# Two broadcast matmuls on 128 rows of the array, later zeroing of the state copies, and an earlier weight load, in a fused linear-attention and SiLU-MLP kernel

## The chip, the cores and the metric

The kernel runs on one core of a Trainium2 chip. The metric is device time in microseconds (us) for one execution of the whole kernel. Times inside an execution come from its hardware profile and count from the start of its span. TensorE is PE in the profile (PEld is its weight load), VectorE is DVE, ScalarE is ACT, GpSimd is POOL, and SyncE, which issues most transfers, is SP. A trailing q (ACTq, POOLq) marks the queue of an engine that issues a DMA.

## The reference, cut to what matters

```
B, H, S, D = 4, 8, 768, 48            # r, k, v: (B, H, S, D); w, u: (H, D)
for t in range(S):
    cur   = outer(u * k[t], v[t])                 # the bonus of the present step
    y[t]  = r[t] @ (state + cur)
    state = w * state + outer(k[t], v[t])         # per head, 48 x 48
x = y with its heads side by side                 # (3072, 384)
h = x @ w_in                                      # w_in  (384, 2048)
out = silu(h) @ w_out                             # w_out (2048, 384)
```

## The kernel before

The sequence of each batch is cut into six chunks of 128 steps. A unit is one chunk of one batch, so there are 24 units; unit i is chunk i // 4 of batch i % 4, and units go in pairs. In a chunk the recurrence becomes matrix products: with powers of w multiplied into r and k, `product_pair` forms the 128 x 128 products of r and k for two units (A01, A23, A45 ...), `masked` cuts them to the past, `outputs_y` multiplies with v and adds the carried state, `outputs_s` forms the chunk's contribution to the state, and `state` adds it.

The powers are made once, at the start. `powers_r` and `powers_k` make lamR and lamK (powers of w along time, with head dimensions as partitions). Two row vectors must be copied to all 128 partitions: the bonus factor u, and w. `spread_u` (L193) and `spread_w` (L189) do it as a matmul of a stationary tile of ones with one row: `ones` is 1 x 128 and the moving operand is the one row `u_row` or `w_row`, so that one row of the PE array takes part. `copy_u` brings the result for u to SBUF as u_bc (L196); `ln_w` and `powers_c` make from that for w the factor lamC, with which `decayed_k` scales k (kc).

The bonus term of unit i is made by a chain over POOL and DVE: `bonus_rk` (rk = k*r, POOL, L222), `bonus_rku` (ru = rk*u_bc, POOL, L227), `bonus_sum` (rd, DVE, L235), `bonus_v` (vu, POOL, L240). `evict_y` (DVE, L345) adds vu to the unit's output.

For the first eight units the order of the work on every engine is written out by hand, in the string `order`: each word is one step of one unit, and each engine takes the words that belong to it in this order. `T` turns r and k of a unit (PE, L262), `kT` and `rT` multiply with the powers (DVE, L268), `A` is the product pair (PE, L295), `am` the masking (DVE, L302), `Y` and `S` the outputs (PE, L312, L317, L329), `yT` and `xT` turn the unit's y, `st` puts the state away (DVE). `La.b` and `Ga.b` are pieces of the first MLP matmul and its SiLU (PE L398, ACT L406) with b the first of the 128-wide column blocks of w_in. A word with `n*` ahead of it puts n matmuls on an idle all-zero tile in front (`spin`, L165), whose results nobody reads.

The MLP weights are loaded by POOL-issued transfers that also convert to f16: `ld_win(g)` (L84, words i_q0 to i_q3) brings the g-th quarter of w_in, which holds column blocks 4g to 4g+3; `ld_wout(g)` (L89, i_o0 to i_o3) a quarter of w_out. POOL takes an issue like any other step, in its place in the order. Quarter 3 is needed first by L4.12. In the order before, this stands around the fourth quarter:

```
rk4 v164 L2.4 G2.4 S2 L2.6 G2.6 st2 ru4 i_q3 r164 L4.8 G4.8 S3 T5 ...
```

DVE clears what needs clearing at the start (L102 to L125): wpT, the idle tile, ones, the pads of the first four rin and kin tiles, and the four f16 copies of the state, st16 (`stb` in the profile). st16 is first written by `state` of unit 0.

All PSUM tiles but the two large `att` ones come from one rotation of four buffers (tag `moe`): each new tile waits until the one four places before it has been read.

## Time and profile before

| | |
|---|---|
| time, median of 3 | 190.74 us (190.19 to 191.87) |
| profiled execution | 193.76 us, span 192.0 us, mean granted TensorE clock 0.973 |
| PE busy | 185.3 us (96%) |
| POOL / ACT / DVE busy | 120.2 / 108.5 / 102.8 us |
| bytes moved | 24.16 MB, mean 126 GB/s |

Engine busy times overlap, so they don't add to the span. A busy PE is one with an instruction in flight; how fast this runs depends on the granted clock, which the profile gives as a share of full speed for any stretch. The page cuts the span into 40 slices of 4.8 us; a window view gives the same numbers for stretches that one chooses.

### The profile page before, as it was taken

Reading aid. Unit: us, or ns where it says so; the run is one execution under the profiler, and the core shown is the slowest. Engines: PE = TensorE matmul, PEld = TensorE weight load, DVE = VectorE, ACT = ScalarE, POOL = GpSimd, SP = SyncE. Lnnn points to the kernel's source line nnn. Section 1 sums busy time; section 2 is a strip of 40 time slices with the busy share of each in tenths; the row PEclk is TensorE's granted clock in tenths of the full one; section 3 lists DMA queues with packets and bytes.
Section 4 is the critical chain, followed back from the end, with each engine's and each line's share of the span. In section 5 each row is a group of like instructions: output and inputs, shape, how many; then the busy total and the mean of one; then the engine's idle time right before and its main releaser. Section 6 shows DMA issues by size and latency. Waiting matters only on the chain.

```text
span 192.0 us, 5629 instructions
## 1 busy us (share of the span) xinstructions
PE 185.3 (96%) x2304; PEld 119.5 (62%) x2304; DVE 102.8 (54%) x188; ACT 108.5 (56%) x213; POOL 120.2 (63%) x159
## 2 busy tenths in 40 slices
PE   7899999799999999999999999999999999999993
PEld 2466676578766876665566655656755657644563
DVE  6556888866772673673673574574574364200120
ACT  5747368769370592276791276791376781089300
POOL 8589699999999939839839839839738430000000
PEclk9856999999999999999999999999999999999999
DMA  5999999999569258278168287177287201320022
GB/s 97 200 196 182 213 144 195 219 180 187 115 144 228 85 112 196 66 162 169 44 121 189 64 178 174 28 144 165 71 177 167 44 0 44 82 82 0 3 82 82
DMA packets 90125, 24.16 MB, mean 126 GB/s; under 512 B 83314, under 2 KB 90100, under 8 KB 90100
## 3 DMA queue, kind: packets, MB, share of 16 engines
q1 hardware_dynamic: 84992, 20.39, 49.2%
q0 software_dynamic: 3712, 3.15, 11.2%
q10 hardware_dynamic: 1396, 0.27, 0.7%
q8 instruction: 18, 0.29, 0.6%
q14 instruction: 7, 0.06, 0.1%
HBM read 20.45 MB, written 4.72 MB: 131 GB/s over the span
## 4 chain that ended last, share of the span: by engine, by line
PE 80%; POOL 8%; DMA 6%; issue 3%; ACT 1%; SPq 1%; DVE 0%; POOLq 0%
PE ops L419 32%; PE hps L398 29%; PE att L295 7%; PE att L262 5%; DMA win<-in_moe_w_in_dram 3%; DMA kin<-in_k_dram 2%; POOL kc L230 2%; PE yp L317 2%; POOL rku_f L227 2%; PE yp L312 2%; POOL vu L240 2%; POOL rk L222 1%; PE ops L444 1%; PE sp L329 1%; POOL win L84 1%
## 5 line engine op out<-in xcount | busy, mean ns | idle before, releaser
L398 PE MATMUL hps<-xT,win 128*128 128x512 f16 (+1 forms) x360 | 67.7, 337 | 1.1 <-DMA win<-in_moe_w_in_dram 1.0
L406 ACT ACTIVATE gT<-hps 128x512 f16<-128x512 f32 x96 | 56.1, 598 | 19.5 <-PE hps L398 17.2
L419 PE MATMUL ops<-wout,gT 128*128 128x384 f16 x368 | 64.0, 326 | 0.0
L398 PEld LDWEIGHTS <-win 128*128 128x128 f16 x360 | 33.3, 98 | 24.8 <-DMA win<-in_moe_w_in_dram 1.2
L419 PEld LDWEIGHTS <-gT 128*128 128x128 f16 x368 | 34.7, 98 | 22.2
L240 POOL TENSOR_TENSOR vu<-vin,rku 128x384 f32<-128x384 f32 x24 | 19.7, 828 | 27.7 <-DVE rku L235 27.7
L425 ACT COPY osb<-ops 128x384 f32<-128x384 f32 x20 | 9.6, 478 | 43.4 <-PE ops L419 39.7
L302 DVE TENSOR_TENSOR am<-att,maskM 128x1024 f16<-128x1024 f32 x12 | 14.7, 1225 | 33.3 <-PE att L295 33.3
L227 POOL TENSOR_TENSOR rku_f<-rk,u_bc 128x384 f32<-128x384 f32 x24 | 23.9, 998 | 3.0 <-ACT u_bc L196 1.3
L222 POOL TENSOR_TENSOR rk<-kin,rin 128x384 f32<-128x384 f32 x24 | 24.1, 1003 | 2.0 <-DMA kin<-in_k_dram 1.9
L230 POOL TENSOR_TENSOR kc<-kin,lamC 128x384 f16<-128x384 f32 x24 | 23.9, 1002 | 0.0
L295 PEld LDWEIGHTS att<-rT,kT 48*64 48x64 f32 x768 | 18.6, 141 | 5.1 <-issue 3.7
L268 DVE TENSOR_TENSOR rT<-att,lamR 112x512 f32<-112x512 f32 x24 | 16.5, 686 | 9.7 <-ACT gT L406 4.0
L345 DVE TENSOR_TENSOR y<-yp,vu 128x384 f16<-128x384 f32 x24 | 13.4, 557 | 14.5 <-issue 4.8
L295 PE MATMUL att<-rT,kT 48*64 48x128 f32 (+1 forms) x768 | 20.5, 257 | 0.5 <-DVE rT L268 0.5
L268 DVE TENSOR_TENSOR kT<-att,lamK 112x512 f32<-112x512 f32 x24 | 16.4, 684 | 4.1 <-PE att L262 4.1
L302 DVE TENSOR_TENSOR am<-att,maskX 128x1024 f16<-128x1024 f32 x12 | 14.6, 1215 | 0.0
L340 POOL TENSOR_TENSOR sdec<-st,wCT 112x384 f32<-112x384 f32 x16 | 13.2, 826 | 0.0
L235 DVE TENSOR_REDUCE rku<-rku_f 128x8 f32<-128x384 f32 x24 | 12.2, 545 | 1.6 <-POOL rku_f L227 1.5
L283 ACT CAST rT<-rT 112x512 f16<-112x512 f32 x20 | 12.4, 619 | 0.1
L427 DVE COPY osb<-ops 128x384 f32<-128x384 f32 x3 | 1.7, 557 | 19.7 <-PE ops L419 19.7
L317 PEld LDWEIGHTS <-am 128*128 128x128 f16 x192 | 10.2, 99 | 3.1 <-DVE am L302 1.1
(67 smaller groups left out, 173.7 us busy)
## 6 DMA issues: line engine op xcount, KB each, us to landing
rin<-in_r_dram SPq DMA_DIRECT2D x24, 192.0 KB, 4.1
vin<-in_v_dram SPq DMA_DIRECT2D x24, 192.0 KB, 4.2
kin<-in_k_dram SPq DMA_DIRECT2D x23, 192.0 KB, 4.0
out_dram<-osb SPq DMA_DIRECT2D x23, 192.0 KB, 2.2
win<-in_moe_w_in_dram POOLq DMA_DIRECT2D x4, 384.0 KB, 6.1
wout<-in_moe_w_out_dram POOLq DMA_DIRECT2D x4, 384.0 KB, 7.5
xT<-y SPq DMA_TRANSPOSE x18, 2.3
kin<-in_k_dram ACTq DMA_DIRECT2D x1, 192.0 KB, 4.1
```

What stands on the lines that cost most here:

```text
L222: nc.gpsimd.tensor_tensor(out=L(i)["rk"], in0=kin[i % NIN][:, :, 0:D], in1=rin[i % NIN][:, :, 0:D], op=ALU.mult)
L227: nc.gpsimd.tensor_tensor(out=L(i)["rku_f"], in0=L(i)["rk"], in1=u_bc, op=ALU.mult)
L230: nc.gpsimd.tensor_tensor(out=kc[i % NIN][:, :, 0:D], in0=kin[i % NIN][:, :, 0:D], in1=lamC, op=ALU.mult)
L240: nc.gpsimd.tensor_tensor(out=L(i)["vu"], in0=vin[i % NIN], in1=L(i)["rku"].unsqueeze(2).broadcast_to([128, H, D]), op=ALU.mult)
L268: nc.vector.tensor_tensor(out=L(i)[key].rearrange("p g (y t) -> p y g t", y=2), in0=L(i)["t"][0:PR, :, x], in1=lam.rearrange("p g (y t) -> ...
L295: nc.tensor.matmul(a[e][o0:o0 + HC, j, p, c0:C], kT[r0:r0 + D, p, s0:s0 + HC], rT[r0:r0 + D, p, c0:C], start=True, stop=True)
L302: nc.vector.tensor_tensor(out=am.rearrange("p h g c -> p (h g) c"), in0=L(i)["a"].rearrange("p h g c -> p (h g) c"), in1=(maskX if crossed ...
L317: nc.tensor.matmul(L(i)["y"][:, h, :], L(i)["am"][:, j, p, :], L(i)["vy"][:, h, :], start=not sc, stop=(not sc or j == 1))
L345: nc.vector.tensor_tensor(out=L(i)["y16"], in0=L(i)["y"], in1=L(i)["vu"], op=ALU.add)
L398: nc.tensor.matmul(hps[:, f, :], win[:, q, (ft + f) * 128:(ft + f + 1) * 128], xts[sc][:, q, b0:b0 + nb, :].rearrange("p b t -> p (b t)"), ...
L406: nc.scalar.activation(out=gts[sc][:, ft:ft + m, b0 * C:(b0 + nb) * C], in_=hpss[b0, ft], func=AF.Silu)
L419: nc.tensor.matmul(opss[b], gts[sc][:, ft, b * C:(b + 1) * C], wout[:, ft, :], start=(ft == 0), stop=(ft == NFT - 1))
```

## The change

There are three parts. The broadcast matmuls use all 128 rows of the array: a tile `rows` of 128 partitions is cleared, the two row vectors are loaded into its partition 0, and `ones` becomes 128 x 128, so that 127 rows add zeros. The clearing of the four st16 tiles moves on DVE from before the exponents (eK) to after them. And the issue of the fourth quarter of w_in (i_q3) moves on POOL ahead of rk4 and ru4, the bonus products of unit 4. The first part is meant to make the broadcasts count as full work of the array, the second to make room on DVE for the larger clear, the third to have the weights there earlier.

```diff
-    w_row = cst.tile([1, HD], FP)
-    u_row = cst.tile([1, HD], FP)
-    ones = cst.tile([1, 128], FP)
+    rows = cst.tile([128, 2, HD], FP)
+    ones = cst.tile([128, 128], FP)
...
     nc.vector.memset(idle, 0.0)
+    nc.vector.memset(rows, 0.0)
...
-    nc.scalar.dma_start(out=u_row, in_=bass.AP(tensor=u.tensor, offset=0, ap=[[0, 1], [1, HD]]))
-    nc.scalar.dma_start(out=w_row, in_=bass.AP(tensor=w.tensor, offset=0, ap=[[0, 1], [1, HD]]))
+    nc.scalar.dma_start(out=rows[0:1, 0, :], in_=bass.AP(tensor=u.tensor, offset=0, ap=[[0, 1], [1, HD]]))
+    nc.scalar.dma_start(out=rows[0:1, 1, :], in_=bass.AP(tensor=w.tensor, offset=0, ap=[[0, 1], [1, HD]]))
...
-    for b in range(B):
-        nc.vector.memset(st16[b], 0.0)
...
     def exponents_k():
         nc.vector.tensor_tensor(out=eK, in0=it_row[:, 1:2, :].broadcast_to([PR, NP, C]),
                                 in1=lnwT.unsqueeze(2).broadcast_to([PR, NP, C]), op=ALU.mult)
+        for b in range(B):
+            nc.vector.memset(st16[b], 0.0)
...
-        nc.tensor.matmul(spread["w"], ones, w_row, start=True, stop=True)
+        nc.tensor.matmul(spread["w"], ones, rows[:, 1, :], start=True, stop=True)
...
-        nc.tensor.matmul(spread["u"], ones, u_row, start=True, stop=True)
+        nc.tensor.matmul(spread["u"], ones, rows[:, 0, :], start=True, stop=True)
...
-        rk4 v164 L2.4 G2.4 S2 L2.6 G2.6 st2 ru4 i_q3 r164 L4.8 G4.8 S3 T5 kT5 rT5 L4.9 G4.9 st3
+        i_q3 rk4 v164 L2.4 G2.4 S2 L2.6 G2.6 st2 ru4 r164 L4.8 G4.8 S3 T5 kT5 rT5 L4.9 G4.9 st3
```

## The prediction
> **What bounds the kernel now.** I read the page's slices first, then the granted clock in chosen windows, then the waits of PE, then the timeline around the one long wait. In the slices PE is at 9 nearly everywhere, but the clock row is not:

> ```profile
> PE   7899999799999999999999999999999999999993
> ...
> PEclk9856999999999999999999999999999999999999
> ```

> So PE bounds the kernel from about 21 us to the end: windows from 45 to 160 us show PE busy in every microsecond, at clock 1.00. Ahead of that lie some 10 us at half clock. Cut at the edges of that stretch, the window view (busy time of PE, PEld, DVE, ACT, POOL, then the clock) says:

> ```profile
> 4.50:7.91 3.41, 2.63 (x35) 1.70 (x35) 1.57 (x3) 3.13 (x13) 2.39 (x7) 1.00 1.06 209
> 7.91:11.32 3.41, 3.41 (x47) 2.18 (x49) 1.56 (x3) 2.32 (x5) 2.13 (x3) 0.51 1.04 204
> 11.32:14.74 3.42, 3.42 (x44) 1.67 (x37) 2.61 (x3) 1.01 (x3) 2.56 (x5) 0.50 1.01 174
> 14.74:18.15 3.41, 3.41 (x35) 2.32 (x33) 2.52 (x5) 2.43 (x6) 3.39 (x4) 0.50 1.07 173
> 18.15:21.56 3.41, 2.93 (x64) 1.88 (x65) 2.21 (x4) 1.74 (x4) 1.84 (x3) 0.99 1.26 229
> ```

> The reader is to see that PE was busy for all of 7.9 to 14.7 us by its records and still did not get its clock back. What it ran then is in the timeline, the one-row broadcasts among it:

> ```profile
> 7.52 1.25 PE L193 MATMUL bc<-u_row,ones 1*128 1x384 f32 x2
> ...
> 12.01 1.64 PE L189 MATMUL bc<-w_row,ones 1*128 1x384 f32 x2
> ```

> PE's own waits are short, and the longest after the opening is for w_in. The clock is full there:

> ```profile
> PE hps L398 <- DMA win<-in_moe_w_in_dram: 1.0, 1, 1.0
> ...
> 29.23 0.80 POOL L84 DMA_DIRECT2D win<-in_moe_w_in_dram  x1
> ...
> 35.95 1.47 PE L398 MATMUL hps<-xT,win 128*128 128x512 f16 x6 [1.03 <-DMA win<-in_moe_w_in_dram]
> ```

> That is L4.12 waiting for quarter 3, issued at 29.23 us and, in the chain of waits, under way for 6.68 us. After it PE waits no more. Hence two places where time can come from: the half-clock stretch, and this one wait. The profiled execution took 193.76 us, the timed median is 190.74; I take differences from the trace and put them on the median.

> [...] half clock from 7.95 to about 18.17 us is 10.2 us, three windows of 3.41, at 0.50. [...]

> **The change part by part.**

> *The larger clear.* From 128 elements at 0.165 and 256 at 0.272 an element costs 0.84 ns; 768 elements of rows are 0.165 + 640 x 0.84 ns = 0.70 us, 0.80 if the 256-element row is tripled. I take 0.75. It sits after idle (ends 1.23), so the pad clears that end near 2.47 end near 3.2. The st16 clears (0.84 us, 2.47 to 3.31) leave this place, so DVE is free at 3.2, as before, and eK, which waits for lnwT and starts at 3.56, does not move. ones grows in rows only: 0.165 as before. The four st16 clears now run after eK, 4.25 to 5.1, where DVE is idle until rT0 at 6.21 (1.95 us idle before it). Cost: nothing, hidden by that idle time. First use of st16 is at 25.93.

> *The new wait.* The two row transfers are issued by ACT and must wait for the clear of rows, to about 2.0 us; they were issued at 1.92. Queued behind them on ACT is lnwT at 3.25, which waits for wpT and had ACT idle 1.16 us. A delay of 0.1 to 0.2 passes at most partly into lnwT, lamR and lamK; lamK ends at 5.34, and rT0 needs it at 6.21. Cost nothing. The rows themselves are needed at 7.52.

> *The matmuls.* Same columns, same two passes each. At equal clock I take the same time, ends 0 and, should rows matter, not above the 1.25 us of the u broadcast.

> *What they do to the clock.* Count, per window, the matmuls that cover the array (spins L165, yp L317, yT L383). The window view by line gives: 11.32 to 14.74, spins 1.01 and yp 0.53, so 1.54 us, clock not restored at its end. 14.74 to 18.15: 1.51 + 0.53 + 0.82 = 2.86, clock restored at its end. With the w broadcast counted in full, the first of these has 1.54 + 1.64 = 3.18, more than what sufficed. So the clock comes back one window earlier, at 14.75. For 7.91 to 11.32, 0.61 of spin plus 0.82 of the u broadcast is 1.43, below the 1.54 that did not suffice; and 4.50 to 7.91 gains only 0.4. Those I leave as they are.

> *What one window is worth.* From 14.75 at full clock: am1 ends at 14.95 in any case, Y1 takes 0.37 in place of 0.53 (the eight at 23.40 show it) and ends near 15.4; T2 takes about 0.8 (its like at 18.47 and 18.74), to 16.2; yT0 and yT1 0.33 each, to 16.75; three spins 0.21 each at full clock, T3 from 17.4. It ran from 18.47 before, so kT3 goes from 19.17 to 18.1. The sum of u products rd2 follows at 19.3 in place of 20.38, POOL is free for vu2 from 19.51, and both PE (A23) and POOL (vu2) move ahead by **1.07 us**. Behind this point both engines run without gaps (PE to 34.92, POOL to 29.23), so it carries on.

> *The fourth quarter.* It moves ahead of two POOL products, 27.22 to 29.23: issue 2.03 us earlier. With the same 6.68 us it lands at 33.9, with the slowest POOL-issued median (7.5 us, w_out) at 34.7; PE comes free at 34.92. The 1.03 us wait is gone. But not all of it is gained. am4 can't begin before A45 ends at 34.92; am4 and am5 hold DVE to 37.33, y4 (0.56) and st4 (0.72) to 38.6. yT4 takes the PSUM buffer that st4 reads, so it can't start before about 38.65; it ran at 39.31. **0.66 us** stay; the bounds are 0.6 and 1.03. rk4 and ru4 end 0.8 us later; rd4, behind them, is held by DVE until 33.91 anyway, and i_o0 is not moved. The other transfers of that time are not needed for several us (r and k of unit 6 issued at 22.43 to 29.26, used at 40.4).

> Sum: 1.07 + 0.66 = 1.73, 190.74 - 1.73 = **189.0 us**.

> **Rivals.**
> - *The broadcasts don't count*[...]. Then only the quarter pays: 190.74 - 0.66 = 190.1. For it: A01, f32 too, filled 2.08 us of an unrestored window. Against: its tiles are 48 x 64, so they are also small.
> - *The clock is never lost.* [...] Then u_bc comes 0.6 us earlier, A01 takes about 1.55 in place of 2.84, am0 and rd1 come about 1.3 earlier, and by the same chain kT3 about 2.9 us earlier than now: 190.74 - 2.9 - 0.66 = 187.2. For it: 18.15 to 21.56 kept its clock with 1.00 us of spins and the A23 tiles. Against: transfers run at about 200 GB/s until 36 us and may hold so early a start.
> - *The half clock lands on dense work.* Faster PE work leaves gaps, [...] the next one, 21.6 to 25, runs the MLP at half clock: 3.41 / 2 = 1.7 lost. PE then reaches L4.12 at 36.6 in place of 35.95, the old wait being swallowed: 190.74 + 0.67 = 191.4, slower than before. Against: the 18.15 window held before with less work.

> **How the numbers follow.** The forecast 0.50, broadcasts don't count 0.25, clock never lost 0.15, half clock on dense work 0.10. The range, 187.2 to 190.8, takes the first three with the 0.6 us of run scatter above the second, and leaves the last out. Faster by over 1% means below 188.83: the clock-never-lost case, and not quite half of the forecast[...], together 0.42. Slower by over 1% is above 192.65, which needs the last case and another lost window: 0.06. Within 1%: 0.52.

> **What would show it.** Right: half clock for two windows (about 6.8 us) or fewer; matmul rows for the broadcasts as long as now at the same clock; no wait of L4.12 for win, and a new short PE wait before yT4 behind st4; kT3 about 1 us earlier. Wrong: three half-clock windows at the same places (the rows don't count), a half-clock slice after 21 us, PE still waiting for win (the transfer is bound by bandwidth, not by its issue), or rT0 later than 6.2 us (the opening pays for the clear).

## The result and the profile after

The changed kernel takes 190.05 us (median of 17 runs, 189.33 to 190.67) against 191.48 us for the kernel before (17 runs, 190.18 to 193.72). The ratio is 0.993, with a 95% interval of 0.9907 to 0.9953. So it is faster by 0.7%, clear of noise and below 1%. The forecast of 189.0 us stood on the first median of 190.74 from three runs; over 17 runs the kernel before is 0.74 us longer than that. Comparisons leave the most disturbed runs out, and here the disturbance is the half clock itself, so over all runs the gain is somewhat larger (below).

The page of the changed kernel, its PE and clock rows over the 40 slices:

```profile
PE   7978899999999999999999999999999999999993
...
PEclk9999999999999999999999999999999999999999
```

The same five windows as before the change, columns as there (length, then busy time of PE, PEld, DVE, ACT and POOL, granted clock, DMA share, GB/s):

```profile
4.50:7.91 3.41, 3.27 (x36) 2.06 (x36) 2.35 (x6) 3.13 (x13) 2.63 (x7) 1.00 1.13 226
7.91:11.32 3.41, 3.38 (x69) 2.01 (x67) 2.22 (x4) 2.53 (x6) 2.54 (x3) 1.00 1.12 221
11.32:14.74 3.42, 2.39 (x42) 1.65 (x43) 3.35 (x6) 2.59 (x5) 3.40 (x5) 1.00 1.00 172
14.74:18.15 3.41, 2.93 (x59) 1.77 (x59) 2.54 (x6) 2.39 (x6) 3.31 (x5) 1.00 1.22 211
18.15:21.56 3.41, 2.63 (x59) 2.13 (x52) 3.21 (x4) 1.19 (x2) 3.39 (x5) 1.00 1.10 198
```

Once full, the clock is not lost again; all 17 runs have a mean clock of 0.998 or 1.0. PE is now idle for 1.0 us in the third window where it had been "busy" throughout: at full clock it runs ahead of DVE there, and the longest wait for am is 0.8 us (below). The views read 1.00 from the start, but for the first microseconds this can hardly be so, by the length of two like groups of matmuls in this trace:

```profile
4.93 0.68 PE L262 MATMUL att<-ident,rin 64*112 64x64 f32 x8
...
6.32 0.43 PE L262 MATMUL att<-ident,rin 64*112 64x64 f32 x8
```

The first took what such a group takes at half clock (0.68 us at 15.62 in the trace before, clock 0.50), the second what it takes at full clock. So the full clock begins near 6 us here, and the mean clock of this run, 1.0, doesn't count the opening ahead of that. The timeline, the same rows as before the change, and two that are new:

```profile
1.34 0.70 DVE L103 MEMSET rows<- 128x768 f32 x1
...
6.14 0.69 DVE L268 TENSOR_TENSOR rT<-att,lamR 112x512 f32<-112x512 f32 x1 [1.06 <-PE att L262]
...
7.21 0.91 PE L193 MATMUL bc<-rows,ones 128*128 128x384 f32 x2
...
10.16 0.91 PE L189 MATMUL bc<-rows,ones 128*128 128x384 f32 x2
...
24.20 0.80 POOL L84 DMA_DIRECT2D win<-in_moe_w_in_dram  x1
...
32.24 1.47 PE L398 MATMUL hps<-xT,win 128*128 128x512 f16 x6
```

The clear of rows takes 0.70 us and rT0 starts no later than before (6.14 against 6.21). The line of the kernel before:

```profile
6.21 0.69 DVE L268 TENSOR_TENSOR rT<-att,lamR 112x512 f32<-112x512 f32 x1 [1.95 <-PE att L262]
```

L4.12, at 32.24 us, has no wait in front of it. The waits of PE in the changed kernel:

```profile
PE yp L317 <- DVE am L302: 1.1, 2, 0.8
PE hps L398 <- DMA win<-in_moe_w_in_dram: 0.8, 1, 0.8
```

The second line is another quarter than before: L0.4 at 21.25 us waits for quarter 1, issued at 14.15, which PE reaches sooner at full clock (the kernel before waits there too when it keeps its clock, 1.19 us in its second trace).

### The profile page after: what moved, and what is told of

Read it like the earlier page. It is cut to its first block, busy times and chain, and to the rows that moved or that the text cites. A ratio compares the mean times of both kernels' runs of the same rounds, so it can differ in the third digit from the quotient of the medians.

```text
span 188.4 us, 5630 instructions
## 1 busy us (share of the span) xinstructions
PE 181.6 (96%) x2304; PEld 117.5 (62%) x2304; DVE 103.2 (55%) x189; ACT 108.4 (58%) x213; POOL 120.1 (64%) x159
## 4 chain that ended last, share of the span: by engine, by line
PE 89%; DMA 4%; POOL 2%; ACT 1%; issue 1%; DVE 1%; DVEq 0%; POOLq 0%
PE hps L398 33%; PE ops L419 32%; PE att L295 8%; PE att L262 6%; DMA win<-in_moe_w_in_dram 4%; PE yp L317 2%; PE yp L312 2%; PE sp L329 2%; PE ops L444 1%; PE att L168 1%; PE zs L163 1%; POOL vu L240 1%; ACT gT L406 1%; POOL rk L222 0%; PE bc L193 0%
## 5 line engine op out<-in xcount | busy, mean ns | idle before, releaser
L398 PE MATMUL hps<-xT,win 128*128 128x512 f16 (+1 forms) x360 | 67.7, 337 | 0.8 <-DMA win<-in_moe_w_in_dram 0.8
L406 ACT ACTIVATE gT<-hps 128x512 f16<-128x512 f32 x96 | 56.0, 598 | 18.7 <-PE hps L398 16.5
L398 PEld LDWEIGHTS <-win 128*128 128x128 f16 x360 | 33.3, 98 | 24.6 <-DMA win<-in_moe_w_in_dram 0.9
L425 ACT COPY osb<-ops 128x384 f32<-128x384 f32 x20 | 9.6, 478 | 43.4 <-PE ops L419 39.7
L302 DVE TENSOR_TENSOR am<-att,maskM 128x1024 f16<-128x1024 f32 x12 | 14.7, 1225 | 31.7 <-PE att L295 31.6
L295 PEld LDWEIGHTS att<-rT,kT 48*64 48x64 f32 x768 | 17.6, 134 | 5.4 <-issue 4.2
L295 PE MATMUL att<-rT,kT 48*64 48x128 f32 (+1 forms) x768 | 19.7, 248 | 0.5 <-DVE rT L268 0.5
L317 PEld LDWEIGHTS <-am 128*128 128x128 f16 x192 | 9.7, 97 | 4.1 <-DVE am L302 2.5
```

What stands on the lines that cost most here:

```text
L295: nc.tensor.matmul(a[e][o0:o0 + HC, j, p, c0:C], kT[r0:r0 + D, p, s0:s0 + HC], rT[r0:r0 + D, p, c0:C], start=True, stop=True)
L302: nc.vector.tensor_tensor(out=am.rearrange("p h g c -> p (h g) c"), in0=L(i)["a"].rearrange("p h g c -> p (h g) c"), in1=(maskX if crossed ...
L317: nc.tensor.matmul(L(i)["y"][:, h, :], L(i)["am"][:, j, p, :], L(i)["vy"][:, h, :], start=not sc, stop=(not sc or j == 1))
L398: nc.tensor.matmul(hps[:, f, :], win[:, q, (ft + f) * 128:(ft + f + 1) * 128], xts[sc][:, q, b0:b0 + nb, :].rearrange("p b t -> p (b t)"), ...
L406: nc.scalar.activation(out=gts[sc][:, ft:ft + m, b0 * C:(b0 + nb) * C], in_=hpss[b0, ft], func=AF.Silu)
```

## The experiments

Each run of a kernel has a mean granted clock, and these fall into a few values only: about 1.0, 0.991, 0.981 and 0.973. With a span near 189 us they are zero, one, two and three stretches of 3.41 us at half clock (half of 3.41 in 189 is 0.009). The traces agree: 0.973 comes with 10.2 us at 0.50 (the kernel before, 7.95 to about 18.17 us), 0.991 with 3.41 us at 0.51 (w on one row, 13.93 to 17.34 us, below); of 0.981 there is no trace. Such a stretch is called a lost window here. The number of runs below 0.995 is therefore the number that lost at least one, and I use it along with the times. For the kernel before, over all 166 runs that lie beside the experiments:

| mean clock | runs | mean time |
|---|---|---|
| 0.998 or more | 69 | 190.53 us |
| 0.99 to 0.991 | 72 | 191.76 us |
| 0.972 to 0.973 | 25 | 193.39 us |
| all | 166 | 191.50 us |

By these means one window costs 1.23 us and three cost 2.86. The profile that the prediction read was one of the 15% with three. "Full-clock mean" below is the mean time of a kernel's runs at 0.995 or more.

### The parts of the change, one at a time

The quarter alone:

```diff
-        rk4 v164 L2.4 G2.4 S2 L2.6 G2.6 st2 ru4 i_q3 r164 ...
+        i_q3 rk4 v164 L2.4 G2.4 S2 L2.6 G2.6 st2 ru4 r164 ...
```

> The kernel before with only the fourth quarter of w_in moved ahead of rk4. Theory (rows count for the clock): the half clock still comes in the opening as it does before, so the mean granted clock is below 0.99 in some runs and the times scatter by 2 to 3 us as before; the wait of L4.12 for w_in is gone and 0.5 to 0.7 us of it stay, so a ratio to before of 0.996 to 0.998. Rival (only the quarter pays, the clock is chance): ratio 0.993 and the times as even as those of the whole change.

Measured: ratio 0.997 (0.9943 to 0.9998). 10 of 22 runs lost the clock, four of them three windows, much as before; times 189.57 to 193.16. Full-clock mean 190.10, which is 0.43 below the 190.53 of before. As the theory had it: the quarter pays, and does nothing for the clock.

All but the quarter (the reverse of the diff above, applied to the changed kernel):

> The whole change but for the quarter, which stays behind ru4. Theory: clock 0.998 to 1.0 in every run, times within about 1.3 us of each other, and a wait of about 0.7 us of L4.12 for w_in in the trace (issue about 26.2 us, 6.7 us under way, PE free at 32.2), of which DVE would have taken a part; ratio to before 0.994 to 0.997. Rival (only the quarter pays): ratio 1.000, clock as uneven as before.

Measured: ratio 0.9938 (0.9915 to 0.9960), none of 22 runs below 0.998, times 189.86 to 191.41. Full-clock mean 190.51, the same as the 190.53 of before: so the larger clear, its wait on ACT and the later st16 clears cost nothing that these means could show (their difference is good to about 0.25 us), and the broadcasts give nothing either where the clock is not lost anyway. The wait of L4.12 was only 0.23 us (of its weight load) in its trace, not 0.7:

```profile
26.23 0.80 POOL L84 DMA_DIRECT2D win<-in_moe_w_in_dram  x1
...
32.27 0.98 PEld L398 LDWEIGHTS <-win 128*128 128x128 f16 x6 [0.23 <-DMA win<-in_moe_w_in_dram]
```

### Is it the rows?

The whole change, its clear, waits and orders included, but one row in both matmuls:

```diff
-        nc.tensor.matmul(spread["w"], ones, rows[:, 1, :], start=True, stop=True)
+        nc.tensor.matmul(spread["w"], ones[0:1, :], rows[0:1, 1, :], start=True, stop=True)
...
-        nc.tensor.matmul(spread["u"], ones, rows[:, 0, :], start=True, stop=True)
+        nc.tensor.matmul(spread["u"], ones[0:1, :], rows[0:1, 0, :], start=True, stop=True)
```

> The whole change, with the larger clear, its wait, the later st16 clears and the earlier quarter, but both broadcast matmuls take only partition 0 of ones and rows, as the kernel before does. Nothing but the number of array rows differs from the whole change. Theory (rows count for the clock): half-clock windows come back, mean clock below 0.995 in four to six of ten runs, as before (34 of 64) and as with the quarter alone (10 of 22); runs at full clock take about 190.0 to 190.1 us. Rival (the later order on DVE and ACT, or the length of the broadcasts, did it): full clock in all runs, times as the whole change.

Measured: ratio 0.9965 (0.9939 to 0.9991), 9 of 22 runs below 0.995, four with three windows; full-clock mean 190.05. That stands against none of 17 for the whole change and none of 22 for the spreads alone, and the edit touches nothing but the rows. The rows decide it here. The runs were made on several chips, but this is no rival: the kernel before lost the clock in 44 of 75 runs beside the one-row runs and in 34 of 64 beside the spreads alone. The edit takes the weight load to one row along with the matmul, so which of the two counts is not shown. The matmul itself is no longer or shorter for them: at full clock the one-row broadcast of u took 0.91 us in the second trace of the kernel before, as the 128-row one does above.

```profile
7.30 0.91 PE L193 MATMUL bc<-u_row,ones 1*128 1x384 f32 x2
```

The broadcasts on 32 rows (`[0:32]` in place of `[0:1]` in the same diff):

> The whole change with the broadcasts on 32 of the 128 rows. [...] a quarter of the rows is nearly as little as one: three to five of ten runs below 0.995. If it asks only for more than some few rows[...], no run below 0.995, as with 128. A step in between, one or two of ten, would say that the measure is graded and 32 rows lie near its bound.

Measured: ratio 0.9955 (0.9930 to 0.9979), 5 of 22 runs below 0.995, one of them three windows. That is apart from 128 rows (0 of 39 in the two kernels above) and not to be told from one row (9 of 22). So 32 did not hold the clock in every run; whether the rows between 1 and 128 make a difference by degrees, these counts don't settle.

### Which broadcast?

w on one row, u on 128 (the first pair of lines of the diff above), and the mirror (the second pair):

> The whole change with only the broadcast of u on 128 rows and that of w on one. Theory: the clock is lost in the gap between the opening spins and A01, in which only the u broadcast lies, so u is the one that holds it: no run, or one in ten, below 0.995. Rival (w matters, as the one that brings a lost clock back a window earlier, which is how the prediction reasoned): about half of the runs below 0.995, in the one-window and the three-window class.

> The mirror: w on 128 rows, u on one. Theory: the clock is still lost in about half of the runs, but comes back sooner, so the three-window class (0.973, a sixth of the runs before) is gone and in its place stand one or two windows (0.991, 0.982). Rival: no run below 0.995.

Measured, w on one row: ratio 0.9962 (0.9937 to 0.9988), 7 of 22 runs below 0.995, all with one window, none with three. Its profile fell on such a run. Cut at the edges of the half-clock stretch, the window view of it:

```profile
10.52:13.93 3.41, 2.45 (x34) 1.09 (x33) 3.34 (x5) 2.56 (x5) 3.39 (x5) 0.99 0.96 179
13.93:17.34 3.41, 3.41 (x35) 2.04 (x31) 1.62 (x3) 2.48 (x6) 3.31 (x5) 0.51 1.10 185
17.34:20.75 3.41, 2.93 (x73) 2.14 (x72) 2.55 (x5) 0.23 (x1) 2.23 (x3) 1.00 1.24 215
```

The 3.41 us ahead of the half clock, 10.52 to 13.93, hold 0.61 us of the one-row w broadcast, 0.98 of spins, 0.75 of yp and a PE wait of 0.78 for am1. My expectation that u alone holds the clock was wrong: 7 of 22 runs lost it with w on one row, 0 of 39 with both on 128. The half clock begins at 13.93 us here and near 7.95 in the first trace of the kernel before. From these two traces I take it, as an estimate, that there are two thin places, one around the u broadcast and one behind A01 with the w broadcast in it. Why a run loses the clock at one, at the other or at neither was not shown.

Measured, u on one row: ratio 0.9962 (0.9941 to 0.9983), one of 22 below 0.995, at 0.981, which is two windows. There the theory held for the three-window class, but far fewer runs lost the clock than the half that I expected. The loss near u, if it is the one with three windows as in that first trace, is the rarer one (25 of 166 runs before had three), and one run in 22 doesn't prove that it is now ended after two windows, though this is what the prediction described.

### Other work in place of rows

The quarter moved, one-row broadcasts as before, and four more spins:

```diff
-        kT0 1*T1 ... v160 v161 1*A01 wb am0 ...
+        kT0 3*T1 ... v160 v161 3*A01 wb am0 ...
```

> The fourth quarter moved, the broadcasts on one row as before, and in their place four more 128x512 matmuls of the idle tile, two ahead of T1 and two ahead of A01 (0.21 us each at full clock, 0.85 us in all[...]). Theory (any matmul that covers the array counts): the clock is held as with the whole change, mean 0.998 to 1.0 in most runs, ratio to before 0.993 to 0.996, somewhat behind the whole change because A01 starts up to 0.4 us later. Rival (it is the broadcasts themselves that matter, for their length or their place): clock below 0.99 as before, ratio 0.997 or above.

Measured: ratio 0.9993 (0.9967 to 1.0019), 7 of 22 below 0.995, all with one window. A half miss: no run has three windows, where the quarter alone had four of 22. This speaks for matmuls of the idle tile counting as the broadcast of u does, but on few runs. None of the four lies near the w broadcast (the last two end before A01 at 8.92, the broadcast starts at 10.42), and one-window losses remain. Full-clock mean 190.29, 0.19 above the quarter alone, which is hardly clear of noise: A01 starts at 8.92 in place of 8.36.

### The quarters

The second quarter ahead of rk2:

```diff
-        lamC 1*Y0 y160 2*Y1 y161 T2 kT2 rT2 rk2 yT0 xT0 yT1 xT1 i_q1 ru2 ...
+        lamC 1*Y0 y160 2*Y1 y161 i_q1 T2 kT2 rT2 rk2 yT0 xT0 yT1 xT1 ru2 ...
```

> The whole change and the second quarter of w_in issued ahead of rk2 in place of behind it. In the trace of the changed kernel L0.4 waits 0.78 us for this quarter at 21.25 us. Theory (PE is the bound from 18.7 us on): issue 0.95 us earlier, this wait gone, and 0.4 to 0.8 us less than the whole change, a ratio to before of about 0.990. Rival (POOL and DVE are the bound there, through kc0 to kc3 and am3, or the landing is set by bandwidth): the same as the whole change, 0.993.

Measured: ratio 0.9931 (0.9900 to 0.9963), mean of 11 runs 190.09 against 189.96 for the whole change: no gain to be seen. In its trace the wait of L0.4 fell from 0.78 to 0.32 us, but the opening was 0.26 us later (L0.0 at 18.96 against 18.70): T0 starts 0.19 us later, and T1's first matmuls take 0.63 us against 0.43, so the half clock of the opening lasted longer there, and the edit, which lies later, can't have done that. And the quarter, issued at 13.46 in place of 14.15, took 7.60 us to the matmul that waited for it in place of 7.10, so most of the earlier issue did not arrive. One trace of each can't say whether that is the rule.

The fourth quarter behind ru5:

```diff
-        i_q3 rk4 v164 ... ru4 r164 ...
-        rd4 rk5 ru5 i_o0 ...
+        rk4 v164 ... ru4 r164 ...
+        rd4 rk5 ru5 i_q3 i_o0 ...
```

> The whole change, but the fourth quarter issued behind ru5, some 2 us later than in the kernel before and 4 us later than in the change. Theory (its landing bounds PE, and DVE bounds what an earlier landing gives): issue near 28.3 us, 6.0 to 6.7 us under way, landing at 34.3 to 35.0 against PE free at 32.1, so a wait of 2.2 to 2.9 us of L4.12 and a time 1.5 to 2.5 us above the whole change, a ratio to before of 0.999 to 1.005. Rival (what follows absorbs such a wait, since the other engines run ahead or POOL is the bound): less than 1 us above the whole change.

Measured: ratio 1.0112 (1.0081 to 1.0144), mean of 22 runs 194.31, that is 4.35 above the whole change, where 1.5 to 2.5 were expected. The wait and what follows, in its timeline and its windows:

```profile
35.43 1.85 PE L398 MATMUL hps<-xT,win 128*128 128x512 f16 x6 [3.51 <-DMA win<-in_moe_w_in_dram]
```

```profile
31.90:35.40 3.50, 0.01 (x3) 0.00 (x0) 2.37 (x3) 1.09 (x3) 3.50 (x5) 1.00 1.19 190
35.40:36.30 0.90, 0.87 (x4) 0.41 (x5) 0.00 (x0) 0.01 (x1) 0.88 (x2) 1.00 1.27 184
36.30:39.70 3.40, 3.40 (x29) 2.06 (x28) 1.17 (x3) 1.33 (x3) 3.31 (x5) 0.51 1.29 218
```

The issue came at 29.14 and not at 28.3. The wait of 3.51 us was followed, 0.9 us after its end, by 3.4 us at 0.51. 17 of 22 runs lost at least one; the five that did not have a mean of 192.75, 2.79 above the whole change. So a wait of PE for this quarter does go into the end time, and is paid a second time where half clock follows it.

### Two more traces

> The whole change with the quarter at its old place, the same code as the run on the spreads alone, for a second trace of the wait of L4.12. In the first the quarter took 6.0 us and L4.12 waited 0.16 to 0.23 us, though runs without the earlier issue are on average 0.5 us longer. If the transfer's time varies from run to run (6.0 to 7 us), this trace shows another wait, up to 1 us; if the wait is the same 0.2 us, the 0.5 us come from elsewhere.

> The kernel before once more, for a second trace. With a mean clock of 1.0 (about half of its runs) its PE should reach the first MLP piece near 18.7 us, as the changed kernel does, with nothing of the 10 us of half clock; with 0.991 it should show one half-clock window of 3.41 us that takes in the w broadcast near 10 us, and PE some 1.3 us behind.

The first (the change without the earlier quarter, clock 1.0, 190.93 us) has no wait of L4.12 but one of 0.65 us of L4.8, for quarter 2, issued at 20.76 and awaited at 27.93. The second (the kernel before, clock 1.0, 190.99 us) waits 1.19 us at L0.4 and 0.40 at L4.12, and reaches L0.0 at 18.79, as the changed kernel does (18.70). One wait of each:

```profile
27.93 0.82 PE L398 MATMUL hps<-xT,win 128*128 128x512 f16 x3 [0.65 <-DMA win<-in_moe_w_in_dram]
```

```profile
33.19 1.47 PE L398 MATMUL hps<-xT,win 128*128 128x512 f16 x6 [0.40 <-DMA win<-in_moe_w_in_dram]
```

So the waits differ between two traces of one kernel: L0.4 none and 1.19 us, L4.12 1.03 and 0.40 in the kernel before; L4.8 none and 0.65 in the change without the earlier quarter. With them differs which quarter PE waits for; a single trace gives this part no size.

## Why the prediction was right

**The total.** Forecast 1.73 us less, measured 1.43 between the medians of 17 runs; over all recorded runs 191.50 - 189.96 = 1.54. The time itself, 190.05, lies 1.05 above the forecast 189.0, and 0.74 of that is the base: three runs gave 190.74 where 17 gave 191.48.

**The clock.** Forecast 1.07 us. Over all runs of before the lost windows cost 191.50 - 190.53 = 0.97, and the change brings all of it. The size was near, the step was not: "So the clock comes back one window earlier" and "Those I leave as they are" are wrong. Once full, the clock is never lost in the changed kernel, which was the rival with 0.15; kT3 comes at 15.87, 3.3 us before its place in the trace that was read, where the forecast had 1.07 and that rival 2.9. I took the one profile for the usual run; it was one of the 15% with three windows. Its 2.9 us put on a median of mixed runs is why that rival's time, 187.2, was too low, and one window on the same median came near by the mixture: 0.42 of the runs had nothing to lose, 0.43 lost one, 0.15 three. That 1.07 met 0.97 is luck. What held is that the rows of these two matmuls count for the clock: with nothing but the rows taken away, the loss came back (0 of 17 runs, then 9 of 22). Nor is the records' busy PE a measure of it: in the trace before, PE was busy for 3.41 of the 3.41 us from 7.91 and from 11.32, at 0.51 and 0.50. The count itself, microseconds of spins, yp and yT per window, was an estimate and did not hold. The window 10.52 to 13.93 of the run with w on one row had 0.98 + 0.75 = 1.73 us, and half clock came after it; the window 18.15 to 21.56 of the trace before had 1.00 of spins, and full clock stayed. The second also holds product-pair matmuls (A23), which the count leaves out; whether a smaller tile counts was not shown.

**The quarter.** Forecast 0.66, with bounds 0.6 and 1.03. Measured at full clock 0.43 (the quarter alone against before) to 0.55 (the whole change against the spreads alone, 190.51 - 189.96), each good to 0.2 or 0.3 us, so 0.66 is too large by little if at all. If it is, the likely reason is that the wait of 1.03 us that it starts from was one draw: 0.40, 0.23 (of the weight load) and none in three other traces. The limit behind it was named as DVE, and the one trace shows a short wait on DVE one step further on: the weight load of yT5 waits for y5, and yT4 does not wait for st4. In the changed kernel:

```profile
36.46 0.21 PEld L383 LDWEIGHTS <-y 128*128 128x128 f16 x3 [0.28 <-DVE y L345]
```

**The clear, its wait and st16.** Forecast nothing; right. The clear took 0.70 us (0.75 forecast, between 0.70 and 0.80 of its two workings), the row transfers were issued at 2.07 in place of 1.92, lnwT stayed at 3.25, rT0 came at 6.14, and the spreads alone at full clock equal the kernel before (190.51 and 190.53).

**The matmuls.** Same time at equal clock: 0.91 us with 1 and with 128 rows. The weight loads hardly differ either: the two of the u broadcast take 0.29 us on one row (the first trace of the kernel before) and 0.30 on 128.

**Rivals.** "The broadcasts don't count" is out by the one-row run. "The half clock lands on dense work" did not happen, but the late quarter shows that it can: 36.3 to 39.7 us at 0.51.

## What to carry to other kernels

Read the granted clock before the busy times, over many runs and not in one profile: in a kernel of this length a mean clock of 0.991 or 0.973 counts the windows lost (3.41 and 10.2 us at half clock in the traces), and the mixture of such runs is what a median changes by. A matmul that keeps PE busy need not hold the clock: here the clock was lost in 9 of 22 runs with the broadcasts on 1 row, in 5 of 22 on 32 and in 0 of 39 padded to 128 with zero rows, at no PE time (0.91 us for the u broadcast on 1 and on 128 rows) and with a clear of 0.70 us that found an idle engine. A wait for a transfer in one trace is one draw. Issuing the fourth quarter earlier gained about half a microsecond where the trace had shown a wait of 1.03, and issuing the second earlier gained nothing to be seen; only runs tell the two apart.
